# The first batch's scan: weight conversions through PSUM, and a chunk's state kept in PSUM, with VectorE in place of GpSimd

## The chip, the cores and the metric

The kernel runs on one core of one Trainium2 chip. The metric is the device time of one execution in microseconds (us), lower is better. The core has five engines with a queue each: TensorE (PE, with its weight loads PEld), VectorE (DVE), ScalarE (ACT), GpSimd (POOL) and SyncE (SP), which issues all DMA here. Each queue runs strictly in the order in which its instructions stand in it.

## The reference

Three blocks one after the other, for 4 batches, 768 tokens, 8 heads of 48:

```python
# attention: a complex decay per head dimension, one state of 48x48 per head
mag = sqrt(a_re**2 + a_im**2); scale = minimum(mag, 0.999) / (mag + 1e-6)
ar, ai = a_re * scale, a_im * scale
for t in range(S):
    S_re, S_im = ar[t]*S_re - ai[t]*S_im + k[t] v[t]^T, ar[t]*S_im + ai[t]*S_re
    y[t] = q[t] @ S_re
# mixer 1: u = x + real(fft(fft(x, tokens), channels)); x = u + relu(norm(u) @ w_ch1) @ w_ch2
# mixer 2: u = x + token MLP(x);  out = u + relu(u @ w_ch1) @ w_ch2
```

## The kernel before

**Batches.** Each batch goes through a *scan* (the running products of the decays, 48 steps outwards from the middle of each of 8 chunks of 96 tokens), a *chunk loop* over the 8 chunks (in `stage1`), the *transform* (`stage2`: folds, mirrors and small matmuls in place of the FFTs, then the normalisation), and the *dense part* (`mlp`, `tok1`, `tok2`; large matmuls). The dense part of one batch runs beside the scan, chunk loop and transform of the next. In the first batch there is nothing dense to run yet: its scan, chunk loop and transform fill the first 181 us, and its first dense matmul (L952) stands behind them. Later batches use other paths in several places (`b == 0` or not).

**The chunk loop.** For chunk c, `ch_u` multiplies the chunk's scaled keys by its values on TensorE into one PSUM bank (16 matmuls, L793 and L794). VectorE then adds the old state T (L804, `Aa`), multiplies the sum by the chunk's real decay (L810, `Xx`), multiplies one half of the rows by the imaginary decay into the other half of `yc` (L811); GpSimd does the other half (L812, on VectorE only for the first chunk, c = 0); and VectorE adds both into the new state T (L814). `ch_sc` makes the scores of the next chunk (L778 on TensorE, masked on VectorE by L785), and `ch_y` the outputs (L827, L833 on TensorE, which needs T of the chunk before), which ScalarE writes to `xT` (L835). `ch_load` fetches the values `V` and keys `Kn` two chunks ahead.

**Conversions.** The weights come as 64-bit floats. `convert` turns one piece of 128x384 into two fp32r pieces and stores them to a scratch area in DRAM, from which later batches load them. Its instructions, in order: a load `cvt<-wL` (L185); on ScalarE the scaled upper word without its sign into the piece `a` (L191) and the scaled lower word (L192); on VectorE a shift of `a` (L194); on GpSimd an addition of the two words (L196); on VectorE the sign, taken from the upper word `hi` (L199); on ScalarE the rounded part (L205); on GpSimd the rest (L206); and a store (L207). All of it lies in SBUF, in buffers of the kind "T", of which there are eight.

**Order.** Of the 56 conversions, 20 run in the first batch, started by `begin` (18 from the chunk loop through `tick`, 2 from `feed` after the transform). `CF` gives how many start at each chunk: pairs up to chunk 3, then eight together at chunk 5, whose loads alone are started there. `rests` puts the VectorE and GpSimd parts of a conversion behind a given instruction of the chunk loop (`tops`, the T of that chunk, and `st["yop"]`, L812), and those in the transform behind its last mirror. The other 36 are started by `lead` in the first batch's dense part. A scheduler that builds the program orders every queue by priority (`RANK`) and by a modelled time; a tile waits until a buffer of its kind is free.

**PSUM.** There are eight banks: three of kind "s", three of "l" and two of "p". The first batch's chunk loop takes "l" for `ch_u` and `ch_y` and "s" for the scores. The two "p" banks hold the running products of a scan; between the first batch's scan and the second batch's nothing lies in them.

Of the kernel before, what the change touches and what calls it, by code (L numbers as in the profile page):

```python
# [8 lines left out]
F32 = mybir.dt.float32  # L9
F32R = mybir.dt.float32r  # L10
I32 = mybir.dt.int32
U32 = mybir.dt.uint32
ACTF = mybir.ActivationFunctionType
ALU = mybir.AluOpType
# [39 lines left out]
def attn_fft_mixer_kernel(ctx: ExitStack, tc: tile.TileContext, aL, xL, vL, wL, qN, kN, vN, arN, aiN,  # L54
# [18 lines left out]
    ve, se, ge = Prio(nc.vector, "v"), Prio(nc.scalar, "v"), Prio(nc.gpsimd, "v")  # L73
    te, sp = Prio(nc.tensor, "pe"), Prio(nc.sync, "sp")
# [17 lines left out]
    def alloc(tag, shape, dt=F32, name=None):  # L92
        n = 1
        for x in shape[1:]:
            n *= x
        t = pool.tile([128, SIZE[tag]], dt, tag=tag, bufs=BUFS[tag], name=name or tag)
        return shaped(t[0:shape[0], 0:n], shape)
# [3 lines left out]
    def palloc(tag, shape):  # L101
        n = 1
        for s in shape[1:]:
            n *= s
        t = psum.tile([128, 512], F32, tag=tag, bufs=PSB[tag], name=tag)
        v = t[0:shape[0], 0:n]
        if len(shape) == 3:
            v = v.rearrange("p (a b) -> p a b", b=shape[2])
        return v
# [7 lines left out]
    ident = misc[:, 0:128]  # L117
# [21 lines left out]
    tiny, shift, top, eps, wee = (lnc[:, j:j + 1] for j in range(5))  # L139
# [25 lines left out]
    def after(x, y):  # L165
        tc.add_manual_dep(x.ins, y.ins.name, HOLD, reason="order of the streams")
# [8 lines left out]
    def rest(x):  # L175

        if rests[0] is not None:
            after(x, rests[0])

    def convert(p, j, w=None, held=True):  # L180


        n = 384
        t = alloc("T", [128, 3 * n], I32, name="cvt")
        x = sp.dma_start(out=t[:, 0:2 * n], in_=wL32[p][:, 768 * j:768 * j + 768])  # L185
        if held:
            hold(x)
        yield
        raw = t[:, 0:2 * n].rearrange("p (n t) -> p n t", t=2)
        lo, hi, a = raw[:, :, 0], raw[:, :, 1], t[:, 2 * n:3 * n]  # L190
        se.activation(out=a.bitcast(F32), in_=hi.bitcast(F32), func=ACTF.Abs, scale=2.0 ** -112)  # L191
        se.activation(out=lo, in_=lo.bitcast(U32), func=ACTF.Copy, scale=2.0 ** -29)  # L192
        yield
        rest(ve.tensor_scalar(out=a, in0=a, scalar1=3, scalar2=None, op0=ALU.logical_shift_left))  # L194
        yield
        x = ge.tensor_tensor(out=a, in0=a, in1=lo, op=ALU.add)  # L196
        if rests[1] is not None:
            after(x, rests[1])
        rest(ve.scalar_tensor_tensor(out=a, in0=hi, scalar=-0x80000000, in1=a, op0=ALU.bitwise_and, op1=ALU.bitwise_or))  # L199
        if w is None:  # L200
            parts = t[:, 0:2 * n].bitcast(F32R).rearrange("p (k n) -> p k n", k=2)
        else:
            yield
            parts = w(p, j)
        se.copy(out=parts[:, 0, :], in_=a.bitcast(F32))  # L205
        ge.tensor_tensor(out=parts[:, 1, :], in0=a.bitcast(F32), in1=r32(parts[:, 0, :]), op=ALU.subtract)  # L206
        sp.dma_start(out=wscr[p][j], in_=r32(parts))  # L207
# [3 lines left out]
    early = [(p, j) for p in range(4) for j in range(2)]  # L211
# [4 lines left out]

    def begin():
        p, j = convs.pop(0)
        return convert(p, j, ws.place if (p, j) in early else None)

    def feed(n):

# [80 lines left out]
    ws = Weights()  # L303
# [415 lines left out]
    def stage1(b):  # L719
# [34 lines left out]
        st = {}  # L754
# [33 lines left out]
        def ch_u(c):  # L788
            d = st[c]
            ps = palloc(PU, [112, 8, 48])  # L790
            for h in range(8):
                vv = d["v"][:, h * 48:h * 48 + 48]
                te.matmul(out=ps[0:64, h, :], lhsT=d["kt"][:, h, 0:64], rhs=vv)  # L793
                te.matmul(out=ps[64:112, h, :], lhsT=d["kt"][:, h, 64:112], rhs=vv)  # L794
            g = gm[b % 2].rearrange("p k (h c) -> p k h c", c=8)[:, :, :, c:c + 1]

            def gb(k, lo, hi):
                return g[lo:hi, k].to_broadcast([hi - lo, 8, 48])

            def v8(ap):  # L800
                return ap.rearrange("p (h e) -> p h e", e=48)
            if c:
                a = alloc("e", [112, 384], name="Aa")
                ve.tensor_tensor(out=v8(a), in0=v8(st["T"]), in1=ps, op=ALU.add)  # L804
                a = v8(a)
            else:
                a = ps
            y = yc[c % 2]
            x = alloc("e", [112, 384], name="Xx")
            ve.tensor_tensor(out=v8(x), in0=a, in1=gb(0, 0, 112), op=ALU.mult)  # L810
            (ge if c and b else ve).tensor_tensor(out=v8(y)[0:48], in0=a[64:112], in1=gb(1, 64, 112), op=ALU.mult)  # L811
            st["yop"] = (ge if c else ve).tensor_tensor(out=v8(y)[64:112], in0=a[0:48], in1=gb(1, 0, 48), op=ALU.mult)  # L812
            T = alloc("e", [112, 384], name="T")
            st["op"] = ve.tensor_tensor(out=T, in0=x, in1=y, op=ALU.add)  # L814
            st["Tn"] = T
            if b == 0:
                tops.append(st["op"])
# [562 lines left out]
```

## Time and profile before

| | |
|---|---|
| median of 3 runs | 1082.09 us (1080.92 to 1084.59) |
| profiled execution | 1079.18 us, span of its instructions 1077.4 us |
| busy share of the span | PE 91%, PEld 85%, DVE 72%, ACT 48%, POOL 39% |
| mean granted TensorE clock | 0.967 of full speed |
| instructions | 21129 |

The profile is of one execution. The span runs from its first instruction to its last; the 1.8 us beside it lie around it. A share of 91% for TensorE is a mean: over the last 697 us it is 97%, over the first 181 us 63%.

### The profile page before, as it was taken

What the parts mean: (1) busy time and instruction counts of PE and PEld (TensorE: products, weight loads), DVE (VectorE), ACT (ScalarE), POOL (GpSimd) and SP (SyncE); (2) the same over time, 40 slices, a digit from 0 to 9 for tenths busy, and PEclk for the clock granted to TensorE, in tenths of its full rate; (3) what the DMA queues carried; (4) which work ended last, traced back from release to release, by engine and by line L of the source; (5) the groups of instructions that cost most, each with busy time, mean ns of one, the idle gap of its engine ahead of it and who ended that gap; (6) DMA issues with size and microseconds to landing.
All of it is one profiled execution on the core that took longest, in us unless ns stands there. A gap on an engine that the chain in (4) does not pass through costs nothing.

```text
span 1077.4 us, 21129 instructions
## 1 busy us (share of the span) xinstructions
PE 979.0 (91%) x7314; PEld 915.2 (85%) x7314; DVE 773.1 (72%) x2121; ACT 511.9 (48%) x1425; POOL 415.1 (39%) x553
## 2 busy tenths in 40 slices
PE   1568787989889999799998999999999999999997
PEld 0338765989789887699998899999889999999997
DVE  6988887989999779899758889874845433433332
ACT  7753445777876226877414667742243212221111
POOL 6635985573586455344336312423622002000000
PEclk9978896999999999899998999999999999999999
DMA  6238843786758646365664256755224434544522
GB/s 222 49 99 240 268 157 120 251 262 188 238 166 288 194 132 193 92 179 167 168 189 142 78 155 196 217 140 149 88 77 158 135 104 147 176 131 132 170 95 76
DMA packets 98337, 173.09 MB, mean 161 GB/s; under 512 B 10928, under 2 KB 57904, under 8 KB 97712
## 3 DMA queue, kind: packets, MB, share of 16 engines
q1 hardware_dynamic: 98224, 171.67, 51.8%
q8 instruction: 60, 0.98, 0.4%
q14 instruction: 53, 0.43, 0.1%
HBM read 132.31 MB, written 39.32 MB: 159 GB/s over the span
## 4 chain that ended last, share of the span: by engine, by line
PE 65%; DVE 18%; POOL 5%; issue 4%; DMA 4%; ACT 3%; SPq 0%; DVEq 0%; POOLq 0%; ACTq 0%
PE l L974 24%; PE l L952 23%; PE s L778 3%; PE s L655 2%; DMA cvt<-wL 2%; DVE cvt L199 2%; PE s L827 2%; POOL cvt L196 1%; PE s L1067 1%; PE s L1042 1%; POOL w L206 1%; PE s L833 1%; PE s L1181 1%; PE s L1199 1%; PE s L793 1%
## 5 line engine op out<-in xcount | busy, mean ns | idle before, releaser
L974 PE MATMUL l<-w,h 128*128 128x384 f32 x1728 | 326.1, 339 | 4.4 <-DVE h L965 2.9
L952 PE MATMUL l<-th,w 128*128 128x384 f32 x1152 | 316.3, 344 | 5.2 <-DVE h L965 4.2
L974 PEld LDWEIGHTS l<-w,h 128*128 128x128 f32 x1728 | 297.1, 188 | 8.8 <-DVE h L965 5.3
L952 PEld LDWEIGHTS l<-th,w 128*128 128x128 f32 x1152 | 212.5, 191 | 8.6 <-DVE h L965 6.3
L952 PE MATMUL l<-tl,w 128*128 128x384 f32 x576 | 196.1, 341 | 0.0
L956 ACT ACTIVATE h<-l 128x384 fp32r<-128x384 f32 x192 | 94.4, 492 | 211.9 <-PE l L952 211.4
L977 DVE TENSOR_TENSOR u<-u,l 128x384 f32<-128x384 f32 x192 | 105.2, 549 | 69.7 <-PE l L974 69.2
L965 DVE SCALAR_TENSOR_TENSOR h<-l,h 128x384 fp32r<-128x384 f32 x160 | 88.5, 554 | 89.6 <-ACT h L956 89.4
L952 PEld LDWEIGHTS l<-tl,w 128*128 128x128 f32 x576 | 110.0, 191 | 0.3 <-DVE tl L936 0.3
L196 POOL TENSOR_TENSOR cvt<-cvt 128x384 int32<-128x384 int32 x56 | 66.0, 1185 | 43.3 <-DVE cvt L194 10.4
L778 PE MATMUL s<-qkt 112*96 112x96 f32 x512 | 58.6, 263 | 9.9 <-DVE sc L785 9.9
L472 PE MATMUL s<-misc,y 128*112 128x128 f32 x96 | 22.4, 382 | 46.3 <-DVE y L450 24.1
L778 PEld LDWEIGHTS s<-qkt 112*96 112x96 f32 x512 | 52.5, 174 | 12.7 <-DVE sc L785 10.9
L472 PEld LDWEIGHTS s<-misc,y 128*112 128x112 f32 x96 | 14.7, 184 | 55.7 <-POOL tm L366 18.9
L1166 POOL TENSOR_TENSOR xl<-u,xh 128x384 fp32r<-128x384 f32 x18 | 18.1, 1013 | 105.8 <-ACT xh L1165 105.8
L206 POOL TENSOR_TENSOR w<-cvt,w 128x384 fp32r<-128x384 f32 x44 | 52.0, 1190 | 8.0 <-ACT w L205 7.7
L199 DVE SCALAR_TENSOR_TENSOR cvt<-cvt 128x384 int32<-128x384 int32 x56 | 45.3, 816 | 5.1 <-POOL cvt L196 4.9
L584 POOL TENSOR_TENSOR tm<-tm 128x144 f32<-128x144 f32 (+1 forms) x51 | 25.3, 497 | 58.9 <-ACT tm L583 58.5
L628 DVE TENSOR_TENSOR p<-p,A 128x144 f32<-128x144 f32 x144 | 44.8, 311 | 2.0
L655 PE MATMUL s<-misc,y 128*112 128x128 f32 x288 | 45.2, 276 | 0.9 <-DVE y L639 0.5
L811 POOL TENSOR_TENSOR yc<-Aa,gm 48x384 f32<-48x384 f32 x18 | 20.6, 1145 | 65.9 <-DVE Aa L804 65.6
L602 POOL TENSOR_TENSOR A<-raw,tm 128x144 f32<-128x144 f32 (+1 forms) x51 | 26.5, 519 | 47.4 <-DVE tm L600 28.5
(222 smaller groups left out, 1961.0 us busy)
## 6 DMA issues: line engine op xcount, KB each, us to landing
w<-wscr SPq DMA_DIRECT2D x180, 384.0 KB, 3.5
cvt<-wL SPq DMA_DIRECT2D x56, 384.0 KB, 4.9
wscr<-w SPq DMA_DIRECT2D x44, 384.0 KB, 3.6
Kn<-kn SPq DMA_DIRECT2D x56, 192.0 KB, 4.2
kn<-y SPq DMA_DIRECT2D x96, 96.0 KB, 2.4
raw<-aL SPq DMA_DIRECT2D x48, 144.0 KB, 3.2
xx<-xL SPq DMA_DIRECT2D x48, 144.0 KB, 3.0
V<-vL SPq DMA_DIRECT2D x32, 144.0 KB, 2.9
```

What stands on the lines that cost most here:

```text
L196: x = ge.tensor_tensor(out=a, in0=a, in1=lo, op=ALU.add)
L199: rest(ve.scalar_tensor_tensor(out=a, in0=hi, scalar=-0x80000000, in1=a, op0=ALU.bitwise_and, op1=ALU.bitwise_or))
L206: ge.tensor_tensor(out=parts[:, 1, :], in0=a.bitcast(F32), in1=r32(parts[:, 0, :]), op=ALU.subtract)
L472: te.transpose(ps[:, j, :], y[:, j, 0:112], ident)
L628: ve.tensor_tensor(out=cur, in0=prev, in1=A[:, j, 0:3, :], op=ALU.mult)
L655: te.transpose(ps[:, j, :], y[:, j, 0:112], ident)
L778: te.matmul(out=ps[:, j, :], lhsT=K[:, hc, :], rhs=Q[:, hc, :])
L952: te.matmul(out=ps, lhsT=w1[:, wi, kt * 128:kt * 128 + 128], rhs=x[g][:, kt, :], start=(n == 0), stop=(n == 8))
L956: x = se.activation(out=hi, in_=ps, func=ACTF.Relu)
L965: ve.scalar_tensor_tensor(out=lo, in0=ps, scalar=0.0, in1=r32(hi), op0=ALU.max, op1=ALU.subtract)
L974: te.matmul(out=ps, lhsT=hs[m][:, hi, tt * 128:tt * 128 + 128], rhs=w2[:, wi, :], start=(n == 0), stop=(n == 8))
L977: ve.tensor_tensor(out=u[tt], in0=u[tt], in1=ps, op=ALU.add)
```

## The change

`begin` asks for conversions with `far=True`. Such a conversion has ScalarE write the scaled upper word, its sign kept, to a PSUM bank of kind "p" in place of `a`; the shift (L194) reads that bank and writes `a` in SBUF, and the sign (L199) is taken from that bank too. The bank is free again after the sign. The 36 conversions of `lead` stay as they are.

In the first batch's chunk loop (c > 0) the old state is added by TensorE: one more matmul of T with the identity (112 rows, 384 columns) goes onto the sum of the 16 products in the bank, whose start and stop flags change for that. `Aa` falls away. Both halves of `yc` are made by VectorE from the bank, then the bank is multiplied by the real decay in place (in place of `Xx`), and T is the sum of the bank and `yc`. GpSimd has no part in the chunk's state any more, and `st["yop"]` is a VectorE instruction. For b > 0 nothing changes.

```diff
-    def convert(p, j, w=None, held=True):
+    def convert(p, j, w=None, held=True, far=False):
...
-        se.activation(out=a.bitcast(F32), in_=hi.bitcast(F32), func=ACTF.Abs, scale=2.0 ** -112)
+        if far:
+            x = palloc("p", [128, n])
+            se.activation(out=x, in_=hi.bitcast(F32), func=ACTF.Copy, scale=2.0 ** -112)
+            top = hi = x.bitcast(I32)
+        else:
+            top = a
+            se.activation(out=a.bitcast(F32), in_=hi.bitcast(F32), func=ACTF.Abs, scale=2.0 ** -112)
...
-        rest(ve.tensor_scalar(out=a, in0=a, scalar1=3, scalar2=None, op0=ALU.logical_shift_left))
+        rest(ve.tensor_scalar(out=a, in0=top, scalar1=3, scalar2=None, op0=ALU.logical_shift_left))
...
-        return convert(p, j, ws.place if (p, j) in early else None)
+        return convert(p, j, ws.place if (p, j) in early else None, far=True)
...
-                te.matmul(out=ps[0:64, h, :], lhsT=d["kt"][:, h, 0:64], rhs=vv)
-                te.matmul(out=ps[64:112, h, :], lhsT=d["kt"][:, h, 64:112], rhs=vv)
+                te.matmul(out=ps[0:64, h, :], lhsT=d["kt"][:, h, 0:64], rhs=vv, start=bool(b or not c or not h), stop=bool(b or not c))
+                te.matmul(out=ps[64:112, h, :], lhsT=d["kt"][:, h, 64:112], rhs=vv, start=bool(b or not c or not h), stop=bool(b or not c))
...
-            if c:
+            if c and b:
                 a = alloc("e", [112, 384], name="Aa")
                 ve.tensor_tensor(out=v8(a), in0=v8(st["T"]), in1=ps, op=ALU.add)
                 a = v8(a)
             else:
                 a = ps
+                if c:
+                    te.matmul(out=ps.rearrange("p h e -> p (h e)"), lhsT=ident[0:112, 0:112], rhs=st["T"], start=False, stop=True)
             y = yc[c % 2]
-            x = alloc("e", [112, 384], name="Xx")
-            ve.tensor_tensor(out=v8(x), in0=a, in1=gb(0, 0, 112), op=ALU.mult)
+            if b:
+                x = alloc("e", [112, 384], name="Xx")
+                ve.tensor_tensor(out=v8(x), in0=a, in1=gb(0, 0, 112), op=ALU.mult)
             (ge if c and b else ve).tensor_tensor(out=v8(y)[0:48], in0=a[64:112], in1=gb(1, 64, 112), op=ALU.mult)
-            st["yop"] = (ge if c else ve).tensor_tensor(out=v8(y)[64:112], in0=a[0:48], in1=gb(1, 0, 48), op=ALU.mult)
+            st["yop"] = (ge if c and b else ve).tensor_tensor(out=v8(y)[64:112], in0=a[0:48], in1=gb(1, 0, 48), op=ALU.mult)
+            if not b:
+                x = a.rearrange("p h e -> p (h e)")
+                ve.tensor_tensor(out=a, in0=a, in1=gb(0, 0, 112), op=ALU.mult)
             T = alloc("e", [112, 384], name="T")
             st["op"] = ve.tensor_tensor(out=T, in0=x, in1=y, op=ALU.add)
```

## Rows read from the trace of the kernel before

**Rows 1.** Stretches: us; busy of PE, PEld, DVE, ACT, POOL; clock; DMA share; GB/s.

```profile
87.00:131.00 44.00, 34.20 (x527) 31.87 (x527) 39.88 (x62) 20.10 (x42) 37.29 (x29) 0.84 0.89 268
145.00:167.00 22.00, 18.94 (x121) 15.16 (x122) 17.79 (x29) 8.75 (x23) 21.31 (x20) 0.97 0.32 127
181.00:380.00 199.00, 186.03 (x1284) 174.92 (x1284) 177.50 (x497) 134.92 (x376) 116.97 (x147) 0.99 0.70 223
...
121.90:130.10 8.20, 7.35 (x60) 6.76 (x60) 8.08 (x13) 5.15 (x11) 8.04 (x7) 0.63 1.03 363
```

**Rows 2.** The chain of waits from 87 to 131 us, shares by line.

```profile
by line: POOL w L206 19.2%; POOL cvt L196 17.0%; issue 12.0%; POOL yc L812 8.9%; DVE T L814 5.4%; POOL cvt L206 5.2%; DVE yc L811 5.0%; DVE Xx L810 4.2%; DVE sc L785 4.0%; POOL qkt L1016 4.0%; DVE cvt L199 2.9%; POOL qkt L1010 2.6%; DVE Aa 
```

**Rows 3.** VectorE's groups, 87 to 131 us: busy us, mean ns; idle before, releaser.

```profile
L811 DVE TENSOR_TENSOR yc<-Aa,gm 48x384 f32<-48x384 f32 x6 | 7.1, 1187 | 0.1
L785 DVE TENSOR_TENSOR sc<-s,misc 96x384 f32<-96x384 f32 x14 | 7.1, 542 | 0.0
L814 DVE TENSOR_TENSOR T<-Xx,yc 112x384 f32<-112x384 f32 x6 | 6.5, 1078 | 2.3 <-POOL yc L812 1.8
L199 DVE SCALAR_TENSOR_TENSOR cvt<-cvt 128x384 int32<-128x384 int32 x10 | 6.2, 624 | 0.9 <-POOL cvt L196 0.9
L810 DVE TENSOR_TENSOR Xx<-Aa,gm 112x384 f32<-112x384 f32 x6 | 6.1, 1023 | 0.1
L194 DVE TENSOR_SCALAR cvt<-cvt 128x384 int32<-128x384 int32 x10 | 4.0, 423 | 0.0
L804 DVE TENSOR_TENSOR Aa<-T,l 112x384 f32<-112x384 f32 x6 | 3.3, 544 | 0.7 <-PE l L794 0.7
```

**Rows 4.** VectorE in order of time (start, us): chunk 0, then chunk 6.

```profile
84.61 0.56 DVE L810 TENSOR_TENSOR Xx<-l,gm 112x384 f32<-112x384 f32 x1 [1.78 <-PE l L794]
...
124.20 0.54 DVE L804 TENSOR_TENSOR Aa<-T,l 112x384 f32<-112x384 f32 x1
126.38 1.35 DVE L810 TENSOR_TENSOR Xx<-Aa,gm 112x384 f32<-112x384 f32 x1
```

**Rows 5.** GpSimd in order of time (start, us): chunk 6 and the transform.

```profile
121.49 3.65 POOL L206 TENSOR_TENSOR w<-cvt,w 128x384 fp32r<-128x384 f32 x2
126.20 1.11 POOL L206 TENSOR_TENSOR cvt<-cvt 128x384 fp32r<-128x384 f32 x1
...
145.30 8.26 POOL L196 TENSOR_TENSOR cvt<-cvt 128x384 int32<-128x384 int32 x6 [4.94 <-DVE cvt L194]
162.40 0.84 POOL L1104 TENSOR_TENSOR qkt<-qkt 128x193 f32<-128x193 f32 x1
169.16 0.53 POOL L1104 TENSOR_TENSOR qkt<-qkt 128x193 f32<-128x193 f32 x1 [2.55 <-ACT qkt L1103]
```

**Rows 6.** VectorE's scan group (before 87 us) that reads and writes PSUM.

```profile
L421 DVE TENSOR_TENSOR l<-l,A 128x96 f32<-128x96 f32 x16 | 4.2, 262 | 0.8 <-ACT ss L436 0.6
```

**Rows 7.** Single lines, first batch: ns min/median/max, first and last start.

```profile
L194 DVE TENSOR_SCALAR cvt<-cvt x20: 341/354/1161, 87.8 to 178.4; 128x384 int32<-128x384 int32 x20
L199 DVE SCALAR_TENSOR_TENSOR cvt<-cvt x20: 543/630/1370, 93.8 to 180.2; 128x384 int32<-128x384 int32 x20
L196 POOL TENSOR_TENSOR cvt<-cvt x20: 1005/1315/2438, 91.0 to 179.0; 128x384 int32<-128x384 int32 x20
L309 PE MATMUL l<-misc x76: 275/275/582, 126.7 to 156.4; 128*128 128x128 f32 x76
L309 PE MATMUL l<-y,misc x16: 592/594/1062, 50.6 to 67.4; 128*128 128x512 f32 x16
```

**Rows 8.** Conversion groups, 131 to 181 us: busy us, mean ns; idle before.

```profile
L196 POOL TENSOR_TENSOR cvt<-cvt 128x384 int32<-128x384 int32 x10 | 12.8, 1299 | 12.6 <-DVE rs L1142 6.6 <-DVE cvt L194 4.9 <-ACT sq L571 1.1
L199 DVE SCALAR_TENSOR_TENSOR cvt<-cvt 128x384 int32<-128x384 int32 x10 | 11.8, 1212 | 3.7 <-POOL cvt L196 3.7
```

**Rows 9.** ScalarE in order of time: one conversion before the transform, one late.

```profile
128.24 0.54 ACT L191 ACTIVATE cvt<-cvt 128x384 f32<-128x384 f32 x1
...
156.81 0.47 ACT L1103 COPY qkt<-s 128x386 f32<-128x386 f32 x1
```

## The prediction

> **What bounds the kernel now.** I read the busy times by stretch first. From 181 us on TensorE is close to its limit: 186.0 of 199 us between 181 and 380 us [rows 1], and more later. The change touches nothing there except through what the first batch leaves behind, so its worth is how much earlier the first 181 us end. Inside them the change works on two stretches. In the chunk loop (87 to 131 us) VectorE is busy for 39.9 and GpSimd for 37.3 of 44 us, TensorE for 34.2 and ScalarE for 20.1; the DMA engines' share is 0.89 at 268 GB/s [rows 1]. So two engines are near full at once, and DMA is not far behind. From 145 to 167 us GpSimd is busy for 21.3 of 22 us [rows 1] with eight conversions.
>
> The chain of waits for the chunk loop says the same: GpSimd's conversion lines (L206, L196) and its `yc` (L812) hold 50% of it (19.2 + 17.0 + 8.9 + 5.2), and VectorE's state lines follow [rows 2]. The groups of instructions show why. Some of VectorE's operations on 384 columns take 0.54 us whatever happens (L785, L804), others have means of 1.02 to 1.19 us (L810, L811, L814) [rows 3]. The difference is in the operands: the first two read one operand from PSUM, the slow three read two from SBUF. In order of time it can be seen at single instructions: at 124.20 us L804 takes 0.54 us while GpSimd is inside a pair of L206 (121.49 to 125.14 us), and at 126.38 us L810 takes 1.35 us beside L206 at 126.20 us [rows 4, 5]. The same L810 in chunk 0, with PSUM as its input and GpSimd idle, took 0.56 us [rows 4]. The conversions show it too: the shift L194 takes 0.34 to 1.16 us, the sign L199 0.54 to 1.37 us, and GpSimd's L196 1.01 us at its shortest and 1.32 us in the median [rows 7]. So the two engines hold each other up through SBUF, and an operand in PSUM escapes that. I take this as a finding of this trace, not as a law.
>
> **The change part by part.** *State of a chunk.* Removed per chunk (c = 1 to 6): L804, L810, L811, L814 at their means, 0.544 + 1.023 + 1.187 + 1.078 = 3.83 us [rows 3]. Put in: two `yc` halves, the multiplication in place and the sum, four operations with one operand in PSUM. The nearest rows are 0.56 us (L810 from PSUM, chunk 0) [rows 4] and 0.544 (L804) [rows 3]; for reading and writing PSUM at once, L421 takes 0.262 us for 96 columns [rows 6]; L804's 0.544 for 384 gives 0.98 ns for each of the 288 further columns, so writing to PSUM costs nothing extra. Four times 0.555 is 2.22 us. Saved: 1.61 us a chunk, 9.7 us over six. The lower bound of the saving is nothing (if the new operations were held up like the old), the upper bound is this.
>
> *The wait between the engines.* L814's wait for GpSimd's L812 (1.8 us in all [rows 3]) goes. In its place VectorE waits for TensorE's addition, which in turn waits for T of the chunk before. That matmul is not in the trace. An identity matmul takes 0.592 us for 512 columns and 0.275 for 128 [rows 7], so 384 columns lie at 0.275 + 256 x 0.000826 = 0.49 us at their shortest, and at most 1.06 us where the clock is low [rows 7]. Queued behind it on TensorE stand the next scores and the outputs; VectorE has the two masks (2 x 0.54 us) and two conversions to do meanwhile, some 3 us a chunk, which covers 0.49 us and its two handovers. If the order in the queue is unlucky the cover is gone and each chunk pays 0.5 to 1.1 us. I charge 0.3 us a chunk, 1.8 us, which cancels the wait that goes.
>
> *Conversions, VectorE.* The sign L199 now reads one operand from PSUM: its mean goes from 0.624 [rows 3] to its shortest, 0.543 us [rows 7]: 0.8 us over ten. The shift L194 is the doubtful one. It reads and writes SBUF now, 0.341 us when nothing disturbs it [rows 7], 0.423 in the mean [rows 3]. Reading PSUM it costs between that 0.341 and L785's 0.542 us; I take 0.54, since L785 is the operation of that size that reads PSUM: 1.2 us more over ten. Together 0.4 us more in this stretch. The Trainium skill ("VectorE: DVE Perf Modes", section "Why PSUM operands drop a tier") says that an operand in PSUM costs a 32-bit operation its double rate. By that rule the shift would be the 0.54 us that I took; were it not so, the sum below would be 2 us better in the chunk loop. No run here shows it yet.
>
> *GpSimd.* L812 leaves it, 6 x 1.03 us (the 8.9% of the chain [rows 2] is part of that), and its own operations lose VectorE as a disturber, L196 falling towards 1.01 us [rows 7].
>
> *Sum for the chunk loop.* VectorE's work shrinks by 9.7 - 0.4 = 9.3 us, from 44 to 34.7 us if it stays as full as now. GpSimd then has 37.3 - 6.2 = 31 us and less, TensorE 34.2 + 6 x 0.49 = 37 us less what its low clock (0.84 in the mean [rows 1]) gives back: for part of the stretch it was granted the lower of its two levels, 1.2 GHz. DMA is the other floor: 44 us at 268 GB/s are 11.8 MB; at 363 GB/s, the rate between 121.9 and 130.1 us [rows 1], they take 32.5 us, and at 0.89 share scaled to full (301 GB/s) 39 us. Not all of these loads are needed in the loop. I put the loop at 36 us: 8 us saved, bounds 4 (DMA or TensorE at 40 us) and 12 (32 us).
>
> *The transform's conversions.* Eight of them run behind the last mirror. The sign's mean there is 1.21 us and L196's 1.30 [rows 8]; without the disturbance ten of the latter save 10 x 0.29 = 2.9 us of GpSimd's 21.3. Against it stands a new wait: before, ScalarE made the upper words of most of them ahead of the transform (the last of a run of four at 128.24 us [rows 9]) and GpSimd could do six additions in a row [rows 5]. Now only two can lie in PSUM, and the third waits until the first has its sign. One round through a bank is copy 0.54 [rows 9], shift 0.54, addition 1.01, sign 0.54 and four handovers, about 3.0 us by these rows with 0.1 us a handover; two banks give one conversion in 1.5 us, and GpSimd needs two operations of 1.0 us for each, 2.0 us. So GpSimd stays the limit and the banks cost one start-up of about 1 to 2 us. Only part of it reaches the end: the first L1104 stood ready when L1103 ended at 157.3 us [rows 9] and came at 162.40, behind conversions [rows 5]; the last one, at 169.16, waited for ScalarE, not for conversions [rows 5]. I count 1.5 us saved, bounds 3 saved and 3 lost.
>
> *The rest* is hidden: GpSimd's freed time outside these stretches, ScalarE's copy to PSUM in place of SBUF (same count, and ScalarE is busy for 20.1 of 44 us [rows 1]). The two last conversions hold "p" banks shortly before the second batch's scan wants them; if they were late, that scan would wait for one round, 3 us.
>
> Sum: 8 + 1.5 = 9.5 us. The profiled execution took 1079.2 us, 2.9 under the median of the runs shown; against the median, 1082.1 - 9.5 = 1072.6 us.
>
> **The rivals.** *(B) Half of it.* DMA or TensorE becomes the floor of the chunk loop at 40 us, and the banks' start-up eats the 1.5 us: 1082.1 - 4 = 1078 us. For it: DMA share 0.89 already, and 1.03 in the last 8 us [rows 1]; against it: the loop needs keys and values, and the conversions' loads can lag.
>
> *(C) Eaten later.* The loop ends earlier, but the dense part of the first batch waits for something with its own pace, so that the end stays: 1081 to 1082 us. For it: TensorE is idle for 13 us between 181 and 380 us [rows 1], where it waits for others; against it: all that it waits for there starts from the same earlier point.
>
> *(D) Slower.* Two banks for a pipeline that kept up to eight conversions open. A copy to PSUM that waits for a bank stands at the head of ScalarE's queue; behind it stand `xT` (L835), which frees the bank that the next products need, and the transform's copies. One exposed round is 3.0 us; with more than three of the nine pairs exposed it outweighs the 9.5 us. All five pairs of the chunk loop: 15 us, less 9.5, 1087 us. For it: the copies' bank is free only after a sign that is ordered behind T of a later chunk; against it: one pair a chunk is exactly the pace of before.
>
> *(E) More.* VectorE stays full, TensorE runs at full clock and DMA lags harmlessly: loop at 32 us and 3 us from the transform, 15 us in all, 1067 us.
>
> **Numbers.** Forecast 0.52, B 0.15, C 0.11, D 0.10, E 0.12. A measurement of this kernel tells about 0.3% from no change, that is 1078.9 to 1085.3 us. Faster: forecast, E and over half of B, 0.73. Same: C and the rest of B, 0.17. Slower: 0.10. The likeliest case alone spans 1068 to 1077 us (loop 4 to 12 and transform within its bounds, the ends not together). The range that leaves out E's far end and D is 1064 to 1083 us.
>
> **What would show it.** Right: L810's successor, L811, L812 and L814 on VectorE at 0.54 to 0.56 us in every chunk; L199 at 0.54; L196 and L206 near 1.0 us; T of chunk 6 about 8 us earlier, and the first dense matmul (L952) some 9 us earlier, with the rest of the trace shifted alike. Wrong: the new operations above 0.8 us (then the operand's place is not what decides); ScalarE or VectorE idle for long behind a bank (D); the DMA share at 1 through the loop with TensorE waiting for `Kn` (B); a first dense matmul 9 us earlier but an end that isn't (C).

## The result and the profile after

The changed kernel takes 1071.61 us in the median of 4 runs (1070.51 to 1072.88), the kernel before 1081.51 us beside it on the same chip (4 runs, 1078.98 to 1084.59): a ratio of 0.9911 with a 95% interval of 0.9885 to 0.9938. The forecast was 1072.6 us. The profiled execution of after took 1071.47 us, its span is 1069.7 us.

In the listing of after the lines stand lower: the conversion is L193 (upper word to its bank), L198 (lower word), L200 (shift), L202 (GpSimd's addition), L205 (sign), L211 and L212 (split); a chunk's state is L815 (TensorE's addition), L820 and L821 (the halves of `yc`), L824 (the multiplication in place) and L826 (T); the scan's mask is L791, `xT` is L847.

I measure four stretches in each profile: the loop from the end of T of chunk 0 to the end of T of chunk 6, the folds and mirrors up to the first shift behind them, the transform from there to the first dense matmul, and the rest. Before they are 43.2, 14.7, 34.9 and 897.7 us; after 37.1, 12.6, 32.1 and 900.1 us. The instructions that set these marks (start, us), first of before, then of after:

```profile
86.33 0.56 DVE L814 TENSOR_TENSOR T<-Xx,yc 112x384 f32<-112x384 f32 x1
128.95 1.18 DVE L814 TENSOR_TENSOR T<-Xx,yc 112x384 f32<-112x384 f32 x1
179.74 0.69 PE L952 MATMUL l<-th,w 128*128 128x384 f32 x1 [0.58 <-ACT th L935]
```

```profile
87.23 0.56 DVE L826 TENSOR_TENSOR T<-l,yc 112x384 f32<-112x384 f32 x1
124.30 0.56 DVE L826 TENSOR_TENSOR T<-l,yc 112x384 f32<-112x384 f32 x1
169.58 1.38 PE L964 MATMUL l<-th,w 128*128 128x384 f32 x3 [1.81 <-ACT th L947]
```

Then the stretches (start and end, length, busy time of PE, PEld, DVE, ACT and POOL, granted clock, DMA share, GB/s): the loop of before, then the loop of after and 20 us of its transform:

```profile
86.90:130.10 43.20, 34.00 (x519) 31.64 (x518) 39.08 (x60) 19.91 (x41) 36.39 (x28) 0.84 0.89 268
```

```profile
87.80:124.90 37.10, 31.98 (x531) 28.02 (x530) 31.26 (x60) 16.70 (x37) 22.86 (x24) 0.99 0.96 284
...
137.40:157.00 19.60, 17.97 (x122) 14.69 (x123) 12.16 (x30) 10.71 (x28) 17.27 (x21) 1.00 0.39 153
```

GpSimd, near full in the loop before, now has 14 us free in it. VectorE is idle for 5.8 us, more than the 4.1 us of the longer loop before. The granted clock of TensorE differs as well, 0.84 before and 0.99 after. The loop does not follow it: in the profiles below it was 39.5 us long at 0.80 (experiment 2), 37.3 us at 0.93 (experiment 5) and 37.1 us at 0.99. The groups of instructions of VectorE in after's loop show both what became shorter and what it waits for (busy us, mean ns, idle time before, releaser):

```profile
L200 DVE TENSOR_SCALAR cvt<-p 128x384 int32<-128x384 int32 x10 | 5.5, 554 | 4.3 <-ACT p L193 4.2
L205 DVE SCALAR_TENSOR_TENSOR cvt<-p,cvt 128x384 int32<-128x384 int32 x10 | 5.1, 546 | 0.0
L820 DVE TENSOR_TENSOR yc<-l,gm 48x384 f32<-48x384 f32 x6 | 3.4, 559 | 1.2 <-PE l L815 1.1
L824 DVE TENSOR_TENSOR l<-l,gm 112x384 f32<-112x384 f32 x6 | 3.3, 558 | 0.0
L826 DVE TENSOR_TENSOR T<-l,yc 112x384 f32<-112x384 f32 x6 | 3.3, 556 | 0.2
L821 DVE TENSOR_TENSOR yc<-l,gm 48x384 f32<-48x384 f32 x6 | 3.3, 550 | 0.1
```

Every operation takes 0.55 to 0.56 us; in [rows 3] three of the four state operations took 1.02 to 1.19 us. New is the first line's wait: 4.2 us in which VectorE stands at a shift until ScalarE's copy to the bank is there. The chain of waits in after's loop says who has taken GpSimd's place:

```profile
by line: DMA cvt<-wL 34.0%; DMA Kn<-kn 18.2%; DVE sc L791 5.0%; PE s L784 5.0%; PE l L839 4.4%; DVE cvt L200 4.3%; DVE yc L820 3.0%; issue 3.0%; DVE yc L821 3.0%; DVE l L824 2.8%; DVE T L826 2.8%; ACT p L193 2.5%; SPq L185 2.3%; PE l L815 2
```

In [rows 2] GpSimd's lines held half of the chain; here the landings of the conversions' loads and of the keys hold it. In order of time, ScalarE and then VectorE around one landing (start, us):

```profile
101.17 0.55 ACT L198 ACTIVATE cvt<-cvt 128x384 int32<-128x384 uint32 x1 [1.10 <-DMA cvt<-wL]
101.63 0.56 ACT L847 ACTIVATE xT<-l,gate 112x384 f32<-112x384 f32 x1
102.09 0.51 ACT L193 ACTIVATE p<-cvt 128x384 f32<-128x384 f32 x1
```

```profile
102.64 0.56 DVE L200 TENSOR_SCALAR cvt<-p 128x384 int32<-128x384 int32 x1 [1.36 <-ACT p L193]
103.22 0.56 DVE L820 TENSOR_TENSOR yc<-l,gm 48x384 f32<-48x384 f32 x1
```

ScalarE waits for the second load with the lower word (L198) at the head of its queue; the upper word (L193), which the shift wants, comes behind it and behind `xT`. On VectorE the chunk's state (L820) stands behind that shift, so the landing of a weight holds up the recurrence.

In the transform the sign (mean 1212 ns in [rows 8]) and GpSimd's addition (1299 ns there) are, after, from 137 to 160 us:

```profile
L205 DVE SCALAR_TENSOR_TENSOR cvt<-p,cvt 128x384 int32<-128x384 int32 x8 | 4.4, 551 | 2.5 <-POOL cvt L202 2.4
```

```profile
L202 POOL TENSOR_TENSOR cvt<-cvt 128x384 int32<-128x384 int32 x8 | 8.2, 1026 | 1.6 <-DVE cvt L200 1.6
```

### The profile page after: what moved, and what is told of

It is laid out like the page before. It is cut to its first block, busy times and chain, and to the rows that moved or that the text cites. A ratio compares the mean times of both kernels' runs of the same rounds, so it can differ in the third digit from the quotient of the medians.

```text
span 1069.7 us, 21120 instructions
## 1 busy us (share of the span) xinstructions
PE 974.0 (91%) x7326; PEld 910.0 (85%) x7326; DVE 760.5 (71%) x2121; ACT 512.1 (48%) x1425; POOL 397.7 (37%) x547
## 4 chain that ended last, share of the span: by engine, by line
PE 68%; DVE 17%; DMA 6%; ACT 4%; issue 3%; POOL 1%; SPq 0%; DVEq 0%; POOLq 0%; ACTq 0%
PE l L986 24%; PE l L964 23%; PE s L784 3%; DMA cvt<-wL 3%; PE s L661 2%; PE s L1079 2%; PE s L1054 2%; PE s L839 2%; DVE cvt L205 1%; PE s L845 1%; PE s L1193 1%; PE s L1211 1%; PE s L799 1%; PE s L944 1%; DVE qkt L1028 1%
## 5 line engine op out<-in xcount | busy, mean ns | idle before, releaser
L202 POOL TENSOR_TENSOR cvt<-cvt 128x384 int32<-128x384 int32 x56 | 59.4, 1064 | 54.1 <-DVE cvt L200 17.9
L784 PE MATMUL s<-qkt 112*96 112x96 f32 x512 | 56.2, 259 | 1.0 <-DVE sc L791 1.0
L212 POOL TENSOR_TENSOR w<-cvt,w 128x384 fp32r<-128x384 f32 x44 | 46.6, 1067 | 18.6 <-ACT w L211 18.3
L634 DVE TENSOR_TENSOR p<-p,A 128x144 f32<-128x144 f32 x144 | 44.6, 310 | 2.1
L820 POOL TENSOR_TENSOR yc<-Aa,gm 48x384 f32<-48x384 f32 x18 | 20.6, 1145 | 65.9 <-DVE Aa L810 65.7
L975 POOL TENSOR_TENSOR h<-full,h 128x384 fp32r<-128x384 f32 x32 | 33.1, 1034 | 31.3 <-ACT full L974 28.4
```

Source lines behind the costliest of these rows:

```text
L634: ve.tensor_tensor(out=cur, in0=prev, in1=A[:, j, 0:3, :], op=ALU.mult)
L784: te.matmul(out=ps[:, j, :], lhsT=K[:, hc, :], rhs=Q[:, hc, :])
L975: ge.tensor_tensor(out=lo, in0=full, in1=r32(hi), op=ALU.subtract)
```

## The experiments

Each ratio is against the kernel before, run beside it on the same chip. Experiments 1 to 4 shared one chip, 5 to 8 another, 9 to 11 a third; 12 had a chip to itself. The stretches, in us, are those of one profile each:

| kernel | ratio, 95% interval | loop | folds | transform | rest |
|---|---|---|---|---|---|
| before | 1 | 43.2 | 14.7 | 34.9 | 897.7 |
| after | 0.9911 [0.9885, 0.9938] | 37.1 | 12.6 | 32.1 | 900.1 |
| 1 state only | 0.9964 [0.9948, 0.9980] | 34.9 | 14.2 | 38.0 | 903.1 |
| 2 conversions only | 0.9931 [0.9908, 0.9955] | 39.5 | 13.6 | 30.4 | 895.3 |
| 3 as 2, `yc` on VectorE | 0.9966 [0.9954, 0.9978] | 41.5 | 12.9 | 30.7 | 900.4 |
| 4 VectorE adds T | 0.9953 [0.9934, 0.9972] | 41.3 | 11.7 | 30.7 | 901.2 |
| 5 after again | 0.9910 [0.9881, 0.9939] | 37.3 | 14.8 | 34.3 | 897.2 |
| 6 loads ahead | 0.9903 [0.9878, 0.9929] | 36.2 | 12.3 | 32.2 | 895.0 |
| 7 banks in the loop alone | 0.9973 [0.9954, 0.9992] | 36.1 | 15.6 | 38.1 | 905.8 |
| 8 banks in the transform alone | 0.9884 [0.9857, 0.9910] | 34.5 | 14.4 | 32.2 | 898.5 |
| 9 copies a chunk later | 0.9983 [0.9963, 1.0002] | 35.6 | 18.6 | 32.1 | 902.8 |
| 10 as 8, copies later | 0.9986 [0.9967, 1.0005] | 34.0 | 20.4 | 32.2 | 898.8 |
| 11 old state, banks in the transform alone | 1.0028 [1.0000, 1.0056] | 44.6 | 15.6 | 30.9 | 906.1 |
| 12 as 8, loads ahead | 0.9931 [0.9910, 0.9953] | 35.4 | 12.3 | 31.7 | 897.4 |

**1. The state alone.** The conversions are as before, the state as after:

```diff
-        return convert(p, j, ws.place if (p, j) in early else None, far=True)
+        return convert(p, j, ws.place if (p, j) in early else None)
```

> The chunk's state in PSUM as changed, the conversions as before, wholly in SBUF. Theory: VectorE and GpSimd hold each other up only where VectorE has two operands in SBUF, so L820 to L826 stay at 0.55 to 0.56 us; the conversions' shift and sign go back to 0.34 to 1.2 and 0.54 to 1.3 us. The chunk loop (T of chunk 0 to T of chunk 6, 43.2 us before, 37.1 us after) stays near 38 us, since DMA sets it; the transform loses its 2.7 us. Total near 1075 us, ratio 0.993 to 0.995 to before. Rival (the two parts only pay together, because a VectorE still slowed by conversions delays the state): loop 41 us or more, ratio above 0.997.

Measured: 1075.93 us, 0.9964. The loop is 34.9 us long, shorter than after's 37.1. VectorE's groups in it:

```profile
L205 DVE SCALAR_TENSOR_TENSOR cvt<-cvt 128x384 int32<-128x384 int32 x10 | 6.8, 692 | 0.1
...
L200 DVE TENSOR_SCALAR cvt<-cvt 128x384 int32<-128x384 int32 x10 | 5.9, 598 | 0.6 <-ACT cvt L197 0.4
L826 DVE TENSOR_TENSOR T<-l,yc 112x384 f32<-112x384 f32 x7 | 3.9, 558 | 0.2
```

The shift and the sign are slower with their operands in SBUF (0.60 and 0.69 us), yet the wait for ScalarE's copy falls from 4.2 to 0.4 us. So the state alone gives all of the loop's gain, the loads do not stop the loop at 37 us, and the transform (38.0 us) gains nothing from it. The median is only 3.9 us below that of before on the same chip: most of the loop's 8.3 us does not reach the end.

**2. The conversions alone.** The bank is used, the chunk's state is the old one (start and stop flags, `Xx` and `yc` too):

```diff
-            if c and b:
+            if c:
                 a = alloc("e", [112, 384], name="Aa")
                 ve.tensor_tensor(out=v8(a), in0=v8(st["T"]), in1=ps, op=ALU.add)
...
-                if c:
-                    te.matmul(out=ps.rearrange("p h e -> p (h e)"), lhsT=ident[0:112, 0:112], rhs=st["T"], start=False, stop=True)
```

> The conversions through PSUM as changed, the chunk's state as before (Aa, Xx, half of yc on GpSimd). Theory: the state's operations with two SBUF operands stay at 1.0 to 1.2 us beside GpSimd, the conversions' shift and sign are at 0.55 us; loop near 41 us, the transform keeps its 2.7 us; total near 1077 us, ratio 0.995 to 0.997. Rival (the conversions were the disturber, the state's place in PSUM is a side matter): loop near 37 us and the ratio of the whole change, 0.991.

Measured: 1070.88 us, 0.9931, more than expected. VectorE's groups in its loop:

```profile
L820 DVE TENSOR_TENSOR T<-Xx,yc 112x384 f32<-112x384 f32 x6 | 8.1, 1356 | 0.1
...
L817 DVE TENSOR_TENSOR yc<-Aa,gm 48x384 f32<-48x384 f32 x6 | 6.2, 1037 | 0.1
...
L200 DVE TENSOR_SCALAR cvt<-p 128x384 int32<-128x384 int32 x10 | 5.4, 545 | 0.0
```

The old state stays slow, and with VectorE that full it never waits for a bank's copy. The transform is the shortest of all, 30.4 us, and the ratio gives 0.69% where the state alone gave 0.36% (the two intervals just overlap).

**3. Both halves of `yc` on VectorE, from SBUF.** To 2 is added:

```diff
-            st["yop"] = (ge if c else ve).tensor_tensor(out=v8(y)[64:112], in0=a[0:48], in1=gb(1, 0, 48), op=ALU.mult)
+            st["yop"] = (ge if c and b else ve).tensor_tensor(out=v8(y)[64:112], in0=a[0:48], in1=gb(1, 0, 48), op=ALU.mult)
```

> As the run with the conversions alone, but both halves of yc are made by VectorE from SBUF: GpSimd has no part in the state, the state's operations still read two operands from SBUF. Theory: Xx, both yc and T remain above 0.8 us in the mean while GpSimd converts, so the loop is not shorter than with the conversions alone, 41 us or more, ratio 0.995 to 0.999. Rival (what cost was the hand-over of L812 to GpSimd and the wait of L814 for it, not the operands' place): loop near 38 us, ratio near 0.992.

Measured: 1075.48 us, 0.9966, and a loop 2 us longer than in 2. VectorE's groups:

```profile
L817 DVE TENSOR_TENSOR yc<-Aa,gm 48x384 f32<-48x384 f32 x6 | 6.2, 1027 | 0.1
L818 DVE TENSOR_TENSOR yc<-Aa,gm 48x384 f32<-48x384 f32 x6 | 6.2, 1026 | 0.1
```

The hand-over to GpSimd is gone and nothing is won: the same two operations take 1.03 us from `Aa` in SBUF and 0.55 from the bank (L820, L821 above). The operand's place is what the state's gain rests on.

**4. VectorE adds the old state into the bank.** One change to after, beside the products' start and stop flags:

```diff
-                    te.matmul(out=ps.rearrange("p h e -> p (h e)"), lhsT=ident[0:112, 0:112], rhs=st["T"], start=False, stop=True)
+                    ve.tensor_tensor(out=ps, in0=v8(st["T"]), in1=ps, op=ALU.add)
```

> As the changed kernel, but VectorE adds the old state into the PSUM bank in place (0.54 us a chunk, one operand in SBUF) and TensorE's matmul with the identity goes. Theory: DMA sets the loop, VectorE has 6 us of idle time there, so 6 x 0.54 = 3.3 us more work is hidden: within 1.5 us of the changed kernel, ratio 0.990 to 0.993. Rival (moving the addition to TensorE is a main part of the gain): 3.3 us slower than the changed kernel, ratio 0.994 or more.

Measured: 1074.72 us, 0.9953, loop 41.3 us. VectorE's groups:

```profile
L200 DVE TENSOR_SCALAR cvt<-p 128x384 int32<-128x384 int32 x10 | 5.3, 551 | 2.6 <-ACT p L193 2.5
...
L815 DVE TENSOR_TENSOR l<-T,l 112x384 f32<-112x384 f32 x6 | 3.3, 553 | 3.9 <-ACT w L211 2.2 <-PE l L800 1.7
```

The six additions cost VectorE 3.3 us and waits of 3.9 us stand before them: together more than the 4.2 us by which the loop is longer than after's. The matmul therefore matters: the loss is the rival's 3.3 us and more, not the hidden one that was expected. How much of it is VectorE's added work and how much the other order of the queues, this run does not separate.

**5. After, once more,** on the chip of 6 to 8.

> The changed kernel once more, beside the next three, so that they can be compared on one chip: ratio to before 0.989 to 0.994, loop (T of chunk 0 to T of chunk 6) 37 us, transform (first shift behind the mirrors to the first dense matmul) 32 us.

Measured: 1070.62 us, 0.9910, as at first. The profile is not the same, though: the first dense matmul comes at 173.6 us, 4.0 us later than in the first profile of the same program. The row that differs most is that from 130 to 140 us, first of after, then of this run:

```profile
130.00:140.00 10.00, 8.06 (x60) 6.45 (x60) 7.45 (x23) 4.93 (x15) 6.92 (x5) 1.00 0.89 308
```

```profile
130.00:140.00 10.00, 7.93 (x37) 5.66 (x38) 7.51 (x19) 3.23 (x8) 3.54 (x5) 0.65 0.82 282
```

The granted clock is 1.00 in one (2.4 GHz) and 0.65 in the other, where a part of the stretch had the lower level. That this clock makes the whole difference is not shown. So two profiles' folds and transforms are alike within some 2 us each, not within tenths; the loops (37.1 and 37.3) agree better.

**6. Two loads ahead.** The conversions are started earlier, in the schedule per chunk:

```diff
-CF = (2, 2, 2, 2, 2, 0, 8, 0)
+CF = (4, 2, 2, 2, 0, 0, 8, 0)
```

> The changed kernel with the conversions started one pair earlier: four before chunk 0, none at chunk 3 (CF = 4, 2, 2, 2, 0, 0, 8, 0). Same work, same bytes. Theory A (the loop waits for the latency of a conversion's load: the load is issued behind xT of a chunk, some 6 us pass, and ScalarE's copy and VectorE's shift stand in their queues until then): VectorE's waits on L193 (4.2 us) go, loop 33 to 35 us, 2 to 4 us faster than the changed kernel. Theory B (the DMA engines' bandwidth sets the loop, share 0.96): loop 37 us as before, no gain.

Measured: 1069.71 us, 0.9903, loop 36.2 us, not to be told from after. Waits in the loop (us in total, times, longest):

```profile
ACT cvt L198 <- DMA cvt<-wL: 11.5, 6, 3.8
...
DVE cvt L200 <- ACT p L193: 3.2, 3, 1.5
```

VectorE's waits, which were to go, fall from 4.2 to 3.2 us. ScalarE still waits for landings, since the copies moved ahead with the loads. The test did not separate a late load from a badly ordered queue.

**7 and 8. The bank in one stretch alone.** `back[2:]` are the conversions of the transform, the rest of `convs` runs in the loop:

```diff
-        return convert(p, j, ws.place if (p, j) in early else None, far=True)
+        return convert(p, j, ws.place if (p, j) in early else None, far=(p, j) in early + back[:2])
```

> The changed kernel, but only the ten conversions of the chunk loop go through PSUM; the ten behind them (in the transform and after it) stay in SBUF as before. Theory: the transform's gain comes from its conversions' signs (1.21 us in SBUF, 0.55 through PSUM) and GpSimd's additions; so the transform is 3 to 5 us longer than in the changed kernel (35 to 37 us against 32), the loop stays at 37 us; ratio 0.993 to 0.996. Rival (two banks cost the transform as much as they give): transform 31 to 33 us, ratio 0.991.

```diff
-        return convert(p, j, ws.place if (p, j) in early else None, far=True)
+        return convert(p, j, ws.place if (p, j) in early else None, far=(p, j) in back[2:])
```

> The opposite: the ten conversions of the chunk loop stay in SBUF, the ten behind them go through PSUM. Theory: with the state in PSUM the loop doesn't need its conversions there (35 us with all of them in SBUF, 37 us through the two banks, where a copy waits for a bank and VectorE for the copy), the transform does: loop 35 us, transform 32 us, 1 to 3 us faster than the changed kernel, ratio 0.987 to 0.990. Rival (the shorter loop of the run with the state alone was luck of that queue order): ratio 0.991 to 0.994.

Measured: banks in the loop alone 1077.90 us, 0.9973; banks in the transform alone 1068.46 us, 0.9884. In the former the transform's conversions show the old trouble (groups of VectorE, then of GpSimd, from 137 to 160 us):

```profile
L205 DVE SCALAR_TENSOR_TENSOR cvt<-cvt 128x384 int32<-128x384 int32 x8 | 10.6, 1357 | 1.8 <-POOL cvt L202 1.8
```

```profile
L202 POOL TENSOR_TENSOR cvt<-cvt 128x384 int32<-128x384 int32 x8 | 10.5, 1339 | 6.2 <-DVE cvt L200 6.2
```

GpSimd's additions take 10.5 us against 8.2 in after, the signs 10.6 against 4.4, and the transform 38.1 against 32.1. Of the latter, ScalarE's and VectorE's groups in the loop:

```profile
L197 ACT ACTIVATE cvt<-cvt 128x384 f32<-128x384 f32 x8 | 4.5, 564 | 10.1 <-DMA cvt<-wL 10.1
L198 ACT ACTIVATE cvt<-cvt 128x384 int32<-128x384 uint32 x8 | 4.4, 550 | 0.0
```

```profile
L200 DVE TENSOR_SCALAR cvt<-cvt 128x384 int32<-128x384 int32 x10 | 6.0, 608 | 0.5 <-ACT cvt L197 0.5
```

ScalarE waits for landings nearly as long as in 6 (10.1 against 11.5 us), but with the upper word at the head of its queue, and VectorE waits for it 0.5 us instead of 4.2. The wait for the landing is still there; who stands behind it has changed.

By the ratios on this one chip, 7 gains 0.27% over before, after (5) 0.90% and 8 1.16%. Taking the bank out of the transform costs 0.63%, some 6.8 us, and the intervals of 5 and 7 lie apart; taking it out of the loop costs nothing.

**9 and 10. Copies one chunk after their load,** first in after, then in 8:

```diff
-                tick(CF[c + 1], c == 5)
+                tick(CF[c + 1], True)
```

> The changed kernel, but a conversion's copies on ScalarE stand one chunk later than its load at every chunk (as they already do for the eight of chunk 5), so the load has landed when ScalarE comes to it. The run with four loads first did not do that: each pair's copies moved along with its load and ScalarE still waited 11.5 us for landings. Theory A (ScalarE's wait at the lower word of a pair's second piece holds the upper words behind it, then the shift on VectorE, then the chunk's state behind the shift): ScalarE's waits for cvt<-wL fall under 4 us, VectorE's on L193 under 1 us, loop 33 to 35 us, ratio 0.986 to 0.989. Theory B (DMA bandwidth): loop 37 us, ratio 0.991.

> The same delay of the copies on the kernel whose chunk loop converts in SBUF and whose transform converts through PSUM (loop 34.5 us, ratio 0.9884). That one's shifts waited only 0.5 us in the loop, so theory A expects little: loop 33.5 to 34.5 us, ratio 0.987 to 0.989. If the loop falls to 32 us or less, ScalarE's waits for the landing (10.1 us there) held the loop in another way, through xT; ratio 0.985.

Measured: 1078.31 us, 0.9983, and 1076.99 us, 0.9986. Neither does what was expected in total. The loops are a little shorter (35.6 and 34.0 us), but the folds grow to 18.6 and 20.4 us. In 9 the wait has not gone either; waits in its loop:

```profile
ACT cvt L198 <- DMA cvt<-wL: 16.3, 10, 3.9
...
DVE cvt L200 <- ACT p L193: 5.3, 1, 5.3
```

The edit moves not only the copies but every later step of a pair by one chunk. So the GpSimd additions and the signs of the last pair come in the folds, where after and 8 have neither. GpSimd and VectorE in the folds of 9, then VectorE in those of 10:

```profile
L202 POOL TENSOR_TENSOR cvt<-cvt 128x384 int32<-128x384 int32 x2 | 3.1, 1568 | 0.0
```

```profile
L205 DVE SCALAR_TENSOR_TENSOR cvt<-p,cvt 128x384 int32<-128x384 int32 x2 | 1.1, 552 | 0.4 <-POOL cvt L202 0.4
```

```profile
L205 DVE SCALAR_TENSOR_TENSOR cvt<-cvt 128x384 int32<-128x384 int32 x2 | 2.6, 1354 | 1.9 <-POOL cvt L202 1.9
```

Part of the shorter loops is therefore work that was put off; whether it accounts for all of the longer folds is not settled. Since ScalarE still waits for landings at the lower words (16.3 us in 9), the case that was to be tested did not come about: these two runs neither show nor refute that a later copy frees the loop.

**11. The old state, banks in the transform alone:** the state's edit of 2 with the condition of 8.

> The chunk's state as before and only the ten conversions behind the chunk loop through PSUM. Theory: the transform's conversions carry most of what the conversions give: transform 31 to 33 us, loop 41 to 43 us as before, ratio 0.992 to 0.995, the same as with all twenty through PSUM (0.9931). Rival (the loop's conversions count as much): ratio above 0.996.

Measured: 1084.19 us, 1.0028. The transform is 30.9 us, near what was expected, the loop 44.6 us, longer than expected, and the first dense matmul comes 1.6 us before that of the kernel before, but the rest of the kernel takes 8 us longer. From 380 to 560 us the rows of before, of 7 and of 11 are:

```profile
380.00:560.00 180.00, 171.17 (x1489) 159.78 (x1486) 149.91 (x456) 102.35 (x311) 78.29 (x119) 0.97 0.54 157
```

```profile
380.00:560.00 180.00, 170.08 (x1340) 156.30 (x1339) 144.87 (x446) 100.34 (x308) 77.05 (x118) 0.91 0.51 150
```

```profile
380.00:560.00 180.00, 170.51 (x1370) 157.01 (x1368) 142.76 (x445) 100.66 (x307) 76.45 (x116) 0.89 0.50 148
```

TensorE is busy for as long, gets through fewer matmuls, and was granted 0.91 and 0.89 in place of 0.97. Kernel 9's profile shows 0.91 there too; the other eleven show 0.96 or 0.97. None of the edits lies in this stretch. It is a matter of the single execution too: the twelve of 11 took 1075.56 to 1090.63 us, the six shorter ones with a mean granted clock of 0.962 to 0.969, the six longer ones with 0.950 to 0.955, and the profile of 7 is of its slowest execution (1083.67 us at 0.957, where its fastest took 1074.79 at 0.971). The 29 executions of before on the chip of 11 had 0.958 to 0.969. So the ratio of 11 contains a clock that its rivals did not have; what its edit is worth at an equal clock, and why it met the lower one so often, stays open.

**12. Banks in the transform alone, and loads ahead:** the diffs of 6 and 8 together.

> The loop's conversions keep their upper words in SBUF, as in the kernel with PSUM only in the transform (loop 34.5 us, ratio 0.9884), and two more of their loads are issued ahead of chunk 1, as in the kernel with loads ahead. If ScalarE's wait for the landings (10.1 us in the loop of the former) still holds the loop's end, the loop falls to 32 to 33 us and the ratio to 0.985 to 0.988. If the landings only fill ScalarE's idle time, now that no copy to a bank stands behind them, the loop stays at 34 to 35 us and the ratio at 0.987 to 0.990.

Measured: 1070.25 us, 0.9931, outside both expectations; the loop of 35.4 us is nearest to the second (34 to 35). Its profiled execution reaches the first dense matmul at 166.7 us, the earliest of all, yet its six runs lie between 1065.87 and 1074.24 us. No gain from earlier loads is shown.

**The best version.** Kernel 8 has the lowest ratio. On its chip its six runs have a median of 1068.46 us (1065.24 to 1070.49), those of after 1070.62 (1068.98 to 1075.93). The ranges overlap and so do the intervals of the ratios; that it beats after is likely, not shown. That it beats before is.

## Why the prediction was right, and where its terms were off

The prediction had the kernel 9.5 us faster; the medians differ by 9.9. To the first dense matmul the profiles' difference is 10.1 us, that is: chunk 0 ends 0.9 us later, the loop is 6.2 shorter (8 forecast, the conversions' waits included), the folds 2.1 shorter (nothing forecast), the transform 2.7 shorter (1.5 forecast). 2.4 us of it are given back later in this profile, 7.7 reach the end of the span. So the total came out by terms that were each off by 1 to 2 us and made up for one another, and that it came out within 0.4 us is luck: the second profile of the same program (experiment 5) reaches its first dense matmul only 6.2 us earlier than before does.

The split of the sum, 8 us for the loop and 1.5 for the transform, is not what the whole times show. The state alone, with the loop at 34.9 us, gives 3.9 us (experiment 1), and the bank in the transform is worth some 6.8 us on top of the rest (5 against 7). What takes the loop's gain away again in 1 and 7 is in part the transform: with no bank there it ran 38.0 and 38.1 us at a granted clock of 0.68, where before had 34.9 us at 0.79. Why the clock is lower there is not shown.

*State of a chunk: right.* Four operations of 0.555 us, 2.22 us a chunk, were forecast; they measure 0.559 + 0.550 + 0.558 + 0.556 = 2.22 us. Writing the bank in place cost nothing. Experiment 3 shows that it is the operand's place: the same work on the same engine from SBUF took 1.03 us. In all fourteen profiles no operation of VectorE on 384 columns with an operand in PSUM took more than 0.57 us in the loop or the transform. Experiment 1 has the whole loop's forecast gain from this step alone, 43.2 - 34.9 = 8.3 us.

*Conversions on VectorE: right.* Forecast 0.54 for the shift and 0.543 for the sign; measured 0.554 and 0.546. The Trainium skill ("VectorE: DVE Perf Modes", section "Why PSUM operands drop a tier") had the shift lose its double rate there; against the 0.341 us of the undisturbed shift from SBUF [rows 7] this trace agrees.

*TensorE's addition: mis-sized.* Forecast 0.49 us from the shortest row of an identity matmul. The trace has two records for each, and a pair runs for 0.90 us:

```profile
99.47 0.90 PE L815 MATMUL l<-T,misc 112*112 112x384 f32 x2 [0.36 <-DVE T L826]
```

The identity rows [rows 7] from which I interpolated count records, not matmuls, so the estimate was about half of the thing. It did no harm: the time charged for waits was 1.8 us, and VectorE waited 1.1 us for L815. Experiment 4 shows that without the matmul the loop is 4.2 us longer.

*ScalarE's copy at nothing: the step that failed.* "The rest is hidden" covered the copy to PSUM with ScalarE's low busy time. Its busy time was no cover: it stands idle in front of a landing, and what is behind it in the queue is late however little it works. With two banks the upper words come behind both lower words, and VectorE waits 4.2 us there. VectorE's work shrank by 39.08 - 31.26 = 7.8 us over the two loops (9.3 forecast), and its idle time grew from 4.1 to 5.8 us, where the sum had let it stay as full. Kernels 1 and 8, which have the new state without the bank in the loop, run it in 34.9 and 34.5 us; 7, which has the bank there, and after run it in 36.1 to 37.3. Kernel 12 (no bank in the loop) with 35.4 and 9 (with it) with 35.6 lie between, so the wait costs the loop at most 3 us, and no closer figure is shown. How much of it the whole kernel pays is not shown either: loop and folds together are 49.7 and 52.1 us in the two profiles of after, 49.1 and 48.9 in those of 1 and 8. With the old state it is the other way round: 39.5 us with the bank (experiment 2) against 43.2 and 44.6 without (before, 11). In the loop the two halves of the change are not additive: alone they take 8.3 and 3.7 us out of it, together 6.2. That both remove the same collisions, and that only the second then pays for its waits, is the likely reason. In the ratios it can't be seen: 0.36% and 0.69% alone, 0.89% and 0.90% together, with intervals too wide to tell that from the sum.

*The floor by DMA (rival B): fell.* The loop was held to be stopped at 39 to 40 us by DMA or TensorE. It ran in 37.1 us at 284 GB/s, and in 34.5 in kernel 8. A lower floor by DMA is not ruled out: the share in after's loop was 0.96, and landings hold half of its chain of waits.

*Transform: right in kind, much too small.* Both mechanisms are there: GpSimd's addition at 1.026 us, the sign at 0.551. The start-up that was to eat half of it shows as 2.1 us of VectorE's idle time and 1.6 us of GpSimd's, so the net was larger than 1.5 us: 2.7 us by the profiles and, as said, some 6.8 us by the ratios of 5 and 7. Where the bank is used the transform takes 30.4 to 34.3 us (eleven profiles), where not 34.9 to 38.1 (before, 1 and 7). That comparison mixes in the granted clock, which from 150 to 180 us was 0.77 in after and 0.53 in experiment 7, and at nearly equal clocks over the whole transform, 0.79 in before and 0.80 in the second profile of after, the lengths are 34.9 and 34.3 us; so of the difference only the 8 x (1.339 - 1.026) = 2.5 us of GpSimd's additions can be put down to the bank here.

*The folds, counted at nothing:* 2.1 us shorter in one profile, 0.1 longer in the other of the same program. They do not simply follow the clock of that stretch: they took 12.6 us at 1.00 and 14.8 us at 0.79 in after's two profiles, but 12.9 us at 0.74 in 3 and 14.2 and 14.4 us at 1.00 in 1 and 8. What sets them stays open, and no term of the change is seen in them.

*Rival C, eaten later:* partly. What is left at the end is the head's gain less or more up to 8 us in the rest of the kernel, which in these fourteen profiles took 895.0 to 906.1 us. *Rival D:* its price did not come. ScalarE waited for a free bank (the sign) 0.7 us in the loop, where the other waits for these copies were for landings, and 3.0 us in the transform, from 137 to 160 us:

```profile
ACT p L193 <- DVE cvt L205: 3.0, 4, 1.2
```

The price of a round had 0.1 us for a hand-over, which no row gave; in the lines above, ScalarE's copy ends at 102.60 us and VectorE's shift starts at 102.64, that is 0.04 us.

## What to carry to other kernels

Where two engines share SBUF and one of them does long operations with two SBUF operands, look at the operand's place before moving work between them: the same operation took 0.55 us from PSUM and 1.03 from SBUF beside a busy GpSimd. A copy that an engine makes "in its idle time" is hidden only if nothing that the critical engine wants stands behind what the idle engine is waiting for; read the order of the queue around a landing, not the busy share. Two edits that remove the same contention should be costed together, and each part run alone: here the version with the lowest time kept the bank only where no recurrence stood behind it, and a gain in one stretch of one profile (8.3 us in experiment 1) came to 3.9 us in the medians of the whole kernel.

## What the runs showed of the hardware that was not expected

The hold-up between VectorE and GpSimd has a size in these rows: for 384 columns VectorE's sign goes from 0.55 to 1.36 us and GpSimd's addition from 1.03 to 1.34 us when both read SBUF alone (after and experiment 7), and no operation of VectorE on 384 columns with an operand in PSUM took more than 0.57 us in the loop or the transform of any of the fourteen profiles.

One program's two profiles differ by 4.0 us at the first dense matmul, with a granted clock of 1.00 in one and 0.65 in the other over the same 10 us; and three of the fourteen profiles show an unedited stretch of 180 us at 0.89 to 0.91 in place of 0.96 to 0.97. Against effects of that size the marks of a single profile show a loop's gain of 6 us, and not the 1 us by which two versions of the transform may differ.
